# Batch one of hash attention plus SwiGLU: scaling, weight steps, hash products and one pair's loads put elsewhere in the order

## The chip, the cores and the metric

The kernel runs on one core of one Trainium2 chip. The metric is the device time of one execution in microseconds (us); the median of three executions of the kernel before is 1002.02 us.

## What is computed

The reference is two blocks in a row. The first is attention in which a query sees only the keys of its own hash bucket (4 batches, 8 heads, 768 positions, head dimension 64):

```python
q_bits = (np.einsum('bhsd,dk->bhsk', q, proj) > 0)      # 6 sign bits, k likewise
mask = q_bucket[:, :, :, None] == k_bucket[:, :, None, :]
scores = np.where(mask, scale * q @ k.T, -1e9)
attn = softmax(scores) @ v
```

The second is a SwiGLU block on x, the attention output as 3072 tokens by 512: `silu(x @ w_gate) * (x @ w_val) @ w_out`, with a hidden width of 1536. The three weight arrays come as 64-bit floats.

## The kernel before, in words

**Rows.** Heads are taken in pairs, so there are 16 pairs, n = 0 to 15, four to a batch. A *row* is half of a pair's 768 queries: row 2n is `half == 0`, row 2n + 1 is `half == 1`. The main loop (L760 to L829) goes through rows. A row has six *score units*, one for each 128 keys: `score` issues the fp32 products of q and k and the bf16 products of the sign bits into two PSUM banks (L485), and ScalarE writes their exponentials (L488). VectorE adds the exponentials up (`add`, five instructions of 128x768 per row, L514 and L518). After the units, `attend` multiplies the exponentials with v (L500) into the one-buffer PSUM tile `av`, and ScalarE copies it to xT (L507).

**Batch one** is rows 0 to 7. They hold attention only. In an even row, `total(n - 1)` comes after the second unit: TensorE sums the accumulators of the pair before into `sum` (L531; in batch one this is the same one-buffer tile as `av`), VectorE takes the reciprocal (L539), and SyncE spreads it over partitions in eight transfers (L544). `norm` then scales xT on VectorE (L551); it waits in the list `waiting`, and `finish(waiting)` issues it after the row's last unit. The next pair is prepared meanwhile by `front(n + 1)`: transposes of k and q (L387, copied by ScalarE, L390), then the *hash products* (`hash_early`, L403), whose signs ScalarE writes (L408: two for q, then four for k, which are kept in `rest` until the row's last unit). The q signs are copied to other partitions by SyncE (`spread_q`, L420: the *signs' transfer*). The hash products are issued in odd rows, after the unit c = NCH - 3 = 3.

**Weights.** The 64-bit weights are turned into fp32 on the chip while attention runs. There are 36 *pieces*: 24 of w_gate and w_val (six blocks of four), then 12 of w_out. A piece is loaded by GpSimd's queue (`load_words`, L273), scaled by ScalarE in two activations (`scale_to`, L288 and L289), and put together by VectorE in three *steps* (L302, L304, L307). After each block come four steps more (`form`, L336), which build Strassen sums; before and after them the block's matrices go to DRAM (L328, L330, L339). Twelve steps at the end build sums of w_out (L359). `prepare_on(count)` takes that many steps of this one sequence. `load_words` keeps at most a few pieces ahead of the last finished one, in buffers that are also used for other things; `scale_ahead` scales at most four pieces ahead.

**Rows 8 and later** (`gating`, from `LATE`) add the SwiGLU block of the batch before, as *atoms*: in rows 8 to 13 each holds 14 atoms, called p0 to p13 here, of two matrix products of about 1.3 us in all (`up`, L575, six PSUM banks). ScalarE takes tanh (`th`, L561), VectorE the gating (L562, L566, L579). `bring` (L318, GpSimd's queue) fetches a block from DRAM at p6, p7, p12 and p13 of each row, once TensorE has left the buffer. Rows 14 and later hold `po` atoms (w_out) as well. Between the atoms of p0 to p8 in general, `prepare_on` takes one step for each.

**Order.** Nothing is scheduled by a planner: each engine runs what is issued to it in the order of this code, and waits on semaphores. The score tiles, the transposes, the hash products and the SwiGLU products share seven PSUM banks in a ring, so that a bank is free again when its reader, seven allocations ago, is done.

Of the kernel before, what the change touches and what calls it, by code (L numbers as in the profile page):

```python
# [18 lines left out]
def kernel(  # L19
# [16 lines left out]
    NCH = S // P  # L36
# [3 lines left out]
    NP = H // 2  # L40
# [36 lines left out]
    def fetch(n, name, queue, half=None):  # L77
        b, pr = pairs[n]
        if name == "v":
            t = raws["v", n] = raw.tile([P, 2, NCH, D], FP32, tag="vraw", name="vraw")  # L80
            queue.dma_start(
                t.rearrange("p h c d -> p h (c d)"),
                v[b, 2 * pr : 2 * pr + 2].rearrange("h (p c) d -> p h (c d)", c=NCH),
            )
            return
        src = q if name == "q" else k
        if not half:
            raws[name, n] = raw.tile([P, NCH, 2, D], FP32, tag=name + "raw", name=name + "raw",
                                     bufs=1)
        t = raws[name, n]  # L90
        if n <= NP:
            cs = slice(None) if half is None else slice(half * CH, (half + 1) * CH)
            for h in range(2):
                queue.dma_start(t[:, cs, h, :],
                                src[b, 2 * pr + h].rearrange("(p c) d -> p c d", c=NCH)[:, cs, :])
            return


        blocks = t.rearrange("p c a b -> p (c a b)").rearrange(
            "p (c a d) -> p c a d", a=P // BLOCK, d=BLOCK)  # L100
        for h in range(2):
            for x in range(D // BLOCK):
                at = h * D + x * BLOCK
                queue.dma_start(  # L104
                    blocks[at : at + BLOCK],
                    src[b, 2 * pr + h][:, x * BLOCK : (x + 1) * BLOCK].rearrange(
                        "(a p c) d -> p c a d", c=NCH, p=BLOCK))

    def load(n, names):
        if n < len(pairs):  # L110
            for name in names:
                fetch(n, name, nc.sync)
# [179 lines left out]
    def scale_ahead():  # L292
        scale_to(min(progress["piece"] + 4, progress["scaled"] + 1))
# [70 lines left out]
    def prepare_on(n):  # L364
        for _ in range(n):
            next(preparing, None)
# [102 lines left out]
    LATE = NP * 2 * NCH  # L469
# [5 lines left out]
    def score(u):  # L475
        n, half, c = units[u]
        qs = slice(half * HQ, (half + 1) * HQ)
        ks = slice(c * P, (c + 1) * P)
        sc = [bank("sc")[:, 0:HQ] for _ in range(2)]
        for x, start in ((T, True), (bits, False)):  # L480
            if u < 2 and not start:
                prepare_pair(1)
            for h in range(2):
                rows = slice(h * D, (h + 1) * D)
                nc.tensor.matmul(sc[h], x["k", n][rows, ks], x["q", n][rows, qs],  # L485
                                 start=start, stop=not start)
        for h in range(2):
            nc.scalar.activation(weights(u)[:, h, 0:HQ], sc[h], AF.Exp,  # L488
                                 scale=SCALE * (OFF / 2 if n <= NP else 1.0))
# [19 lines left out]
    def add(u):  # L509
        n, half, c = units[u]  # L510
        a = weights(u)
        if c == 1:
            acc[n, half] = att.tile([P, 2, HQ], FP32, tag="acc", name="acc")
            nc.vector.scalar_tensor_tensor(out=acc[n, half], in0=weights(u - 1)[:, :, 0:HQ],  # L514
                                           scalar=S * EPS / P, in1=a[:, :, 0:HQ],
                                           op0=ALU.add, op1=ALU.add)
        elif c > 1:
            nc.vector.tensor_tensor(acc[n, half], acc[n, half], a[:, :, 0:HQ], op=ALU.add)  # L518

    def total(n):  # L520

        b, pr = pairs[n]

        ps = av_ps.tile([P, 512], FP32, tag="av", name="sum") if b == 0 else bank("sum")
        t = [acc.pop((n, half)) for half in range(2)]
        for h in range(2):
            for half in range(2):
                g = (2 * h + half) * BLOCK  # L530
                nc.tensor.matmul(ps[g : g + BLOCK, 0:HQ], ones, t[half][:, h, :],  # L531
                                 start=True, stop=True)
        if b == 0:
            space = wo.rearrange("p f m -> p (f m)")
            space = space[:, n % 2 * 3 * HQ : (n % 2 + 1) * 3 * HQ].rearrange("p (x q) -> p x q", q=HQ)
            r, t = space[:, 2, :], space[:, 0:2, :]
        else:
            r, t = t[1][:, 0, :], t[0]
        nc.vector.reciprocal(r, ps[:, 0:HQ])  # L539
        for half in range(2):  # L540
            for h in range(2):
                g = (2 * h + half) * BLOCK
                for at in (h * D, h * D + BLOCK):
                    nc.sync.dma_start(t[at : at + BLOCK, half, :], r[g : g + BLOCK, :])  # L544
        waiting.append(lambda: norm(n, t))
        if pr == NP - 1:
            push_ffn(b)
# [198 lines left out]
    rest = []  # L746

    def prepare_pair(count):
        for _ in range(count):
            rest.extend(f for f in steps.pop(0)() or [] if f)  # L750

    def finish(todo):
        while todo:
            todo.pop(0)()
# [5 lines left out]
    for u in range(0, N, NCH):  # L760
        n, half, _ = units[u]
        gating = u >= LATE
        if u == MOVE:
            progress["late"] = True
            for t in late_ring:
                nc.gpsimd.memset(t[:, :, HQ:AW], 1.0)
        for c in range(NCH):
            score(u + c)
            if u + c == 2 or not gating and half == 1 and c == NCH - 3:
                prepare_pair(1)  # L770
            if c == 1 and half == 0 and 0 < n <= NP:
                total(n - 1)
            if c:
                add(u + c)
        if n <= NP:
            finish(waiting)
            finish(rest)
        if not gating and half == 0:
            steps = front(n + 1)
        if not gating and half == 0 and u > 0:  # L780
            prepare_pair(2)
        for _ in range(1 if u else 2):
            scale_ahead()
        for c in range(NCH):
            attend(u + c)
        if not gating:
            scale_ahead()
        if half == 1:
            load(n + 2, "qkv" if gating else "v")
        elif not gating:  # L790
            prepare_pair(2 if u > 0 else 4)
            load(n + 2, "qk")
        finish(first)
        prepare_on(0 if u == LATE else 4)
        chores = []
        if half == 1 and n >= NP:
            total(n)
            if n + 1 < len(pairs):
                chores = [None] + steps.pop(0)()
        prepare_on(0 if LATE - NCH <= u <= LATE else 3)  # L800
        if not gating:
            continue
        if n + 1 < len(pairs) and half == 0:
            steps = front(n + 1)
            chores = [None, steps.pop(0), None, steps.pop(0)]

        credit += 14 if n < 2 * NP else 15.75
        end = True
        part = 0
        while atoms and (credit > 0 or not end):  # L810
            size, atom, end = atoms.pop(0)
            credit -= size
            atom()
            part += size
            if part >= 11 or u + NCH == N and part >= 6:
                finish(waiting)
                if u + NCH == N:
                    finish([first.pop(0) for _ in range(min(2, len(first)))])
            if 5 < part < 14 if u == LATE else part < 9:
                prepare_on(size)  # L820
            if 6 < part < 11 or u == LATE and part > 10:
                scale_ahead()
            for _ in range(size):
                if chores:
                    step = chores.pop(0)
                    chores.extend(step and step() or [])
        while chores:
            step = chores.pop(0)
            chores.extend(step and step() or [])  # L829
# [34 lines left out]
```

## Time and profile before

| what | us |
|---|---|
| median of 3 executions (1001.76 to 1002.82) | 1002.02 |
| the profiled execution | 1002.31 |
| its span from first to last instruction | 1000.3 |
| TensorE busy | 990.2 (99%) |
| VectorE busy | 570.7 (57%) |
| ScalarE busy | 398.4 (40%) |
| GpSimd busy | 101.5 (10%) |

The granted TensorE clock is full throughout. Shares of the whole span are averages over stages: attention alone lasts until about 114 us, weights are prepared until about 288 us, and after that VectorE is around half busy. The end of a matrix product is modelled in the profile, and a product that is held up is often shown as a longer one; lengths of whole stages tell more than the idle time.

### The profile page before, as it was taken

To read this page: it belongs to the slowest core of one execution; us is meant where nothing else is said; L and a number is where in the kernel's file an instruction comes from. 1 tells how busy PE (TensorE), PEld (TensorE's weight loads), DVE (VectorE), ACT (ScalarE), POOL (GpSimd) and SP (SyncE) were. 2 spreads that over 40 slices of the span, in tenths; PEclk is the share of its full clock that TensorE was granted. 3 is DMA by queue.
4 is the path that set the end of the run, shared out by engine and by line. 5 is a ranking of instruction groups with operands and counts; after the bars stand their busy time and mean duration, and the time that the engine had idled before them with its cause. 6 is when DMAs were issued, how large, how long until landed. Compare 5 with 4: busy or idle time off the path is not lost.

```text
span 1000.3 us, 12465 instructions
## 1 busy us (share of the span) xinstructions
PE 990.2 (99%) x4597; PEld 599.8 (60%) x4597; DVE 570.7 (57%) x892; ACT 398.4 (40%) x885; POOL 101.5 (10%) x200
## 2 busy tenths in 40 slices
PE   9999999999999999999999999999999999999998
PEld 4444455555576765555557775555556786555687
DVE  5888998887873624556564443554556442435431
ACT  6988555465323214444342223334343211222200
POOL 3222022221000000000000000000000000111000
PEclk9999999999999999999999999999999999999999
DMA  7777595885213032333331204333122012323001
GB/s 230 214 252 244 146 259 161 216 291 148 76 43 76 22 96 84 87 100 95 97 103 34 69 17 116 92 90 100 44 84 77 22 38 64 105 82 111 29 27 37
DMA packets 120749, 106.95 MB, mean 107 GB/s; under 512 B 89264, under 2 KB 104080, under 8 KB 120688
## 3 DMA queue, kind: packets, MB, share of 16 engines
q0 software_dynamic: 19104, 73.28, 22.9%
q1 hardware_dynamic: 100784, 32.67, 14.3%
q8 instruction: 36, 0.59, 0.3%
q10 hardware_dynamic: 800, 0.20, 0.1%
q14 instruction: 25, 0.20, 0.1%
HBM read 81.79 MB, written 17.30 MB: 99 GB/s over the span
## 4 chain that ended last, share of the span: by engine, by line
PE 87%; DMA 2%; DVE 1%; SPq 1%; ACT 1%; issue 1%; POOL 0%; DVEq 0%; POOLq 0%
PE up L575 43%; PE po L575 22%; PE sc L485 12%; PE av L500 9%; PE sum L531 1%; DMA words<-in_moe_w_out_dram 1%; PE hps L403 1%; SPq L104 1%; DMA wo<-wo 1%; DMA qb<-qb 0%; DMA room<-ram 0%; DVE room L359 0%; ACT A L488 0%; DVE wo L539 0%; DVE acc L518 0%
## 5 line engine op out<-in xcount | busy, mean ns | idle before, releaser
L575 PE MATMUL up<-xT,room 128*128 128x384 f32 x768 | 260.9, 488 | 0.0
L575 PEld LDWEIGHTS up<-xT,room 128*128 128x128 f32 x768 | 144.6, 190 | 106.7 <-issue 9.8
L575 PE MATMUL up<-xc,room 128*128 128x384 f32 x576 | 197.4, 486 | 0.0
L485 PE MATMUL sc<-qT,kT 64*128 64x384 f32 x768 | 161.5, 494 | 0.2 <-DVE c L562 0.2
L575 PEld LDWEIGHTS up<-xc,room 128*128 128x128 f32 x576 | 109.5, 190 | 76.3
L579 DVE TENSOR_TENSOR c<-c,up 128x384 f32<-128x384 f32 x72 | 39.8, 553 | 180.1 <-PE up L575 179.7
L518 DVE TENSOR_TENSOR acc<-acc,A 128x768 f32<-128x768 f32 x128 | 122.7, 958 | 14.4 <-ACT A L488 1.0
L318 POOL DMA_DIRECT2D room<-ram x96 | 52.4, 546 | 714.3 <-PE up L575 707.2
L488 ACT ACTIVATE A<-sc 128x384 f32<-128x384 f32 x256 | 105.6, 499 | 3.5 <-PE sc L485 3.4
L485 PEld LDWEIGHTS sc<-qT,kT 64*128 64x128 f32 x768 | 67.8, 186 | 55.5 <-issue 45.7
L710 ACT COPY o<-po 128x256 f32<-128x256 f32 x48 | 17.9, 372 | 200.5 <-PE po L575 200.5
L561 ACT ACTIVATE th<-c 128x384 f32<-128x384 f32 x72 | 37.6, 522 | 128.7 <-DVE c L562 89.2
L500 PE MATMUL av<-A,vraw 128*64 128x384 f32 (+1 forms) x512 | 88.2, 486 | 0.0
L579 DVE TENSOR_TENSOR o<-o,po 128x256 f32<-128x256 f32 x36 | 15.2, 421 | 111.6 <-PE po L575 82.5
L485 PE MATMUL sc<-qb,kb 64*128 64x384 bf16 x384 | 65.4, 323 | 1.7 <-DMA qb<-qb 1.2
L488 ACT ACTIVATE room<-sc 128x384 f32<-128x384 f32 x128 | 54.0, 495 | 32.6 <-PE sc L485 32.6
L575 PE MATMUL po<-wo,hid 128*128 128x256 f32 x288 | 66.9, 382 | 0.0
L575 PE MATMUL po<-wo,room 128*128 128x256 f32 x288 | 66.3, 379 | 0.1
L575 PE MATMUL po<-room,hid 128*128 128x256 f32 x288 | 66.1, 379 | 0.0
L500 PEld LDWEIGHTS av<-A,vraw 128*64 128x64 f32 x512 | 36.7, 137 | 46.0 <-issue 44.1
L638 ACT COPY c<-up 128x384 f32<-128x384 f32 x72 | 34.4, 478 | 69.1 <-PE up L575 69.1
L575 PEld LDWEIGHTS po<-wo,hid 128*128 128x128 f32 x288 | 54.1, 190 | 12.1 <-issue 4.9
(110 smaller groups left out, 969.4 us busy)
## 6 DMA issues: line engine op xcount, KB each, us to landing
room<-ram POOLq DMA_DIRECT2D x48, 512.0 KB, 4.8
room<-ram POOLq DMA_DIRECT2D x48, 384.0 KB, 3.9
vraw<-in_v_dram SPq DMA_DIRECT2D x16, 384.0 KB, 3.3
ram<-room POOLq DMA_DIRECT2D x12, 512.0 KB, 4.8
out_dram<-o SPq DMA_DIRECT2D x48, 128.0 KB, 1.7
room<-in_moe_w_out_dram POOLq DMA_DIRECT2D x10, 512.0 KB, 6.3
qraw<-in_q_dram SPq DMA_DIRECT2D x48, 96.0 KB, 3.2
hid<-in_moe_w_gate_dram POOLq DMA_DIRECT2D x9, 512.0 KB, 6.9
```

Of the source, the lines that this page charges most:

```text
L104: queue.dma_start(blocks[at : at + BLOCK], src[b, 2 * pr + h][:, x * BLOCK : (x + 1) * BLOCK].rearrange("(a p c) d -> p c a d", c=NCH, p=B ...
L318: nc.gpsimd.dma_start(places[k % 2][:, PARTS[go], :], ram[k % NG][:, PARTS[go], :])
L403: nc.tensor.matmul(tile_[i * BLOCK : (i + 1) * BLOCK, 0:HQ], hash_w, T[name, n][:, half * HQ : (half + 1) * HQ], start=True, stop=True)
L485: nc.tensor.matmul(sc[h], x["k", n][rows, ks], x["q", n][rows, qs], start=start, stop=not start)
L488: nc.scalar.activation(weights(u)[:, h, 0:HQ], sc[h], AF.Exp, scale=SCALE * (OFF / 2 if n <= NP else 1.0))
L500: nc.tensor.matmul(ps[h * D : (h + 1) * D, 0:width], raws["v", n][:, h, c, :], a[:, h, 0:width], start=c == 0, stop=c == NCH - 1)
L518: nc.vector.tensor_tensor(acc[n, half], acc[n, half], a[:, :, 0:HQ], op=ALU.add)
L561: nc.scalar.activation(th, g, AF.Tanh, scale=0.5)
L575: nc.tensor.matmul(ps, a, x, start=start and i == 0, stop=i == len(pairs_) - 1, skip_group_check=True)
L579: nc.vector.tensor_tensor(o, a, b, op=op)
L638: nc.scalar.copy(tile_of(g, spot), c)
L710: nc.scalar.copy(o, c)
```

## The change

Four things move, three of them in batch one.

1. `norm` (L551) of pairs 0, 1 and 2 is issued after the last unit of the odd row that follows its reciprocal, and no longer after that of the same even row. Pair 3's stays in row 8.
2. The second `prepare_on` of rows 1, 3 and 5 takes one step and no longer three: six steps fewer before row 8. In row 11 and later rows of the weights' preparation, steps are taken between the atoms p0 to p9 and no longer p0 to p7. Every step of the sequence, with its loads and scalings, comes later by six in rows 6 to 10; the six are made up two each in rows 11, 12 and 13.
3. The hash products and the q signs of rows 1, 3, 5 and 7 are issued after the third unit and no longer after the fourth.
4. The q and k loads of the sixth pair (n = 5; four transfers each) are issued in row 7, after the signs' transfer of pair 4 and just ahead of that pair's v load, and no longer in row 6.

```diff
         for c in range(NCH):
             score(u + c)
-            if u + c == 2 or not gating and half == 1 and c == NCH - 3:
+            if u + c == 2 or not gating and half == 1 and c == 2:
                 prepare_pair(1)
...
-        if n <= NP:
+        if half == 1 and n < NP or u == LATE:
             finish(waiting)
-            finish(rest)
+        finish(rest)
...
         if half == 1:
-            load(n + 2, "qkv" if gating else "v")
+            load(n + 2, "qkv" if n + 2 > NP else "v")
         elif not gating:
             prepare_pair(2 if u > 0 else 4)
-            load(n + 2, "qk")
+            if n + 2 <= NP:
+                load(n + 2, "qk")
...
-        prepare_on(0 if LATE - NCH <= u <= LATE else 3)
+        prepare_on(0 if LATE - NCH <= u <= LATE else 3 if gating or not half else 1)
...
-            if 5 < part < 14 if u == LATE else part < 9:
+            if 5 < part < 14 if u == LATE else part < (9 if u < LATE + 3 * NCH else 11):
                 prepare_on(size)
```

## The prediction

> **What bounds the kernel now.** I read the page first, then TensorE's timeline up to 320 us by rows, then what VectorE, ScalarE and the queues did where a row was longer than its like. TensorE is busy for 99% of the span, so only its stalls can be won. Its rows have fixed lengths when nothing holds them: a score stage of 36 records takes 5.05 us in the chain, an `av` stage 4.03, `sum` 0.78, an `up` stage 18.26. In batch one an odd row takes 10.85 us each time. An even row should take 10.75 (1.72 for two units, 0.78, 3.43 for four, 0.80, 4.03). The timeline (start, length, what; idle before it in brackets) gives three places:
>
> ```profile
> 62.79 1.52 PE L500 MATMUL av<-room,vraw 128*64 128x386 f32 x8 [1.67 <-DVE wo L539]
> ...
> 87.27 1.52 PE L500 MATMUL av<-room,vraw 128*64 128x386 f32 x8 [1.38 <-DVE wo L539]
> ...
> 104.41 0.32 PE L485 MATMUL sc<-qb,kb 64*128 64x384 bf16 x1 [1.17 <-DMA qb<-qb]
> ```
>
> Row 2 (31.50 to 42.60) is 0.36 over, row 4 (53.45 to 66.83) 2.63, row 6 (77.68 to 91.31) 2.88; row 8 has 1.6 too much before its `av` (109.68). In all **7.5 us**. Rows 4 and 6 are long since `sum` waits for the last addition of the row before, and `av` for the reciprocal that frees its bank. Busy times in the windows row 2+3, 4+5, 6+7 (PE, PEld, DVE, ACT, POOL):
>
> ```profile
> 31.50:53.45 21.95, 21.80 (x150) 10.12 (x148) 17.75 (x23) 20.18 (x46) 6.95 (x12) 1.00 0.69 211
> 53.45:77.68 24.23, 22.51 (x150) 10.25 (x148) 20.74 (x27) 20.17 (x46) 5.38 (x9) 1.00 0.79 265
> 77.68:102.17 24.49, 22.70 (x151) 10.26 (x149) 21.93 (x27) 20.26 (x46) 8.32 (x14) 1.00 0.85 256
> ```
>
> TensorE could do a pair in 21.6. VectorE's 20.7 to 21.9 plus its waits don't fit. Its timeline has hardly a gap from 28 to 114 us, but for `norm`, issued before its transfers land:
>
> ```profile
> 59.57 0.69 DVE L307 CUSTOM_DVE_ANT_0 room<-hid,room 128x1024 uint16<-128x1024 uint16 x1
> 60.18 2.55 DVE L539 RECIPROCAL wo<-sum 128x384 f32<-128x384 f32 x1
> ...
> 70.04 1.02 DVE L551 SCALAR_TENSOR_TENSOR xT<-xT,e,wo 128x768 f32<-128x768 f32 x1 [2.25 <-DMA wo<-wo]
> ```
>
> Later, two more stalls: row 12 begins its `av` 1.06 us late, row 13 0.9. ScalarE stood before a w_out piece, and the tanh behind it held VectorE's last bank release:
>
> ```profile
> 216.18 0.67 ACT L288 ACTIVATE wo<-words 128x512 f32<-128x512 f32 x1 [1.77 <-DMA words<-in_moe_w_out_dram]
> ...
> 244.45 0.67 ACT L288 ACTIVATE wo<-room 128x512 f32<-128x512 f32 x1 [2.79 <-DMA room<-in_moe_w_out_dram]
> 245.57 0.51 ACT L561 ACTIVATE th<-c 128x384 f32<-128x384 f32 x1
> ```
>
> **What the skill says.** The Trainium skill's Perfetto Trace Analysis, "Tensor Engine Instruction", says that ScalarE, VectorE and GpSimd work strictly first in, first out; the trace agrees: the tanh above starts right after the scaling it has nothing to do with. Its "Identifying the Most-Contended Engine" warns that matmul busy time misleads; here the stall of 7.5 us in batch one shows as under 5 us of idle time. DMA: Bandwidth & Descriptors, "Issuing engines are not separate DMA queues", says that transfers of all queues share 16 engines; in the trace a 512 KB w_out load takes 5.5 to 7.5 us by what else runs.
>
> **Batch one, step by step.** Slot lengths from VectorE's timeline (start to start): a piece's three steps 1.79, a form step 0.70, the additions of a row 5.1, reciprocal 2.47, `norm` 0.93.
>
> *Steps and `norm`.* Row 1 now ends VectorE's work at 34.34 without two form steps, so the reciprocal of row 2 follows `sum` at 34.4 and not at 35.67. Additions end at 41.9, four form steps and a piece at 46.5, row 3's additions (bound by the exponentials) at 52.1, `norm` without a wait (transfers landed near 44) at 53.0, five steps at 56.0. Before, row 3's additions ended at 55.9 and seven steps stood between them and the reciprocal at 60.18. Now row 4's `sum` waits only for ScalarE's xT copy (55.3), and the reciprocal runs from 56.2 to 58.7, ahead of `av` at 60.4. Row 4's stall falls from 2.63 to 0.2: **2.4**. The same walk through rows 5 and 6: row 6 starts at 75.3, additions of row 5 end at 73.4, `sum` at 77.0, reciprocal to 80.5 against an `av` at 82: **2.9** gone. `norm` is a move within VectorE: 0.93 less in the even row, 0.93 more in the odd one, and the waits of 2.37, 2.25 and 1.46 go. Its reader is the SwiGLU in row 8; nothing waits in between. Six steps less are 6 x 0.6 = 3.6 us of VectorE.
>
> *Hash products.* Two signs (1.15 us of ScalarE) and four products change places with one unit; no work is added. ScalarE has the q sides copied by then (in row 3: 45.0 against products at 45.95). The bank ring lets the products take the bank of a finished transpose; the next row's first unit gets their bank, and needs the k signs anyway. The cost is nothing, as ScalarE's exponentials run behind TensorE by less than the ring allows (0.4 us to spare at the tightest); without that, up to 0.6 in each odd row, the products' time.
>
> *Loads.* In row 6 the eight loads held SyncE's queue from 92.46 to 99.08, and the signs' transfer came at 99.59, landing 4.77 later. Now SyncE is free after the eight `wo` transfers, the signs come 0.8 earlier, and row 8 finds them. The eight issues go behind, some 6.6 us, with v behind them: from 91.7 to 98.7 on the new clock, landed by 102. Pair 5 is transposed near 113 there, its v is used in row 10, and the next `wo` transfers are due at 102.6. Row 8's 1.6 is gone: **1.6**. Sum of batch one **6.9, taken as 6.8** (bounds 4 and 7.5).
>
> **The price later.** Rows 8 to 10 take as many steps as before, only others, and their ends had slack: the last gating ends before TensorE asks for its bank (row 10's tanh starts 15.5 us after `up` began, and 17.6 is where a stall begins, by rows 12 and 13). Each w_out piece now stands where the piece two places earlier stood.
>
> *Row 10* scales piece 24 last. Its load waits for the block's DRAM copies and should be issued at 178.5, landing 6.3 to 7.5 later; tanh at 186.8 against a limit of 187.5. Cost 0 (0 to 1.0).
>
> *Row 11* scales piece 28 last. Its load stands behind `bring` on GpSimd's queue, as piece 30's did, and also behind the last block's copies, which start 6 us later than before. I get an issue at 208.9 against 208.68. Cost 0.2 (-0.3 to 1.5).
>
> *Row 12* ends with piece 34; before with 35. The lines of GpSimd's queue:
>
> ```profile
> 236.58 0.53 POOL L318 DMA_DIRECT2D room<-ram  x1 [6.86 <-PE up L575]
> 237.11 0.53 POOL L273 DMA_DIRECT2D room<-in_moe_w_out_dram  x1
> 237.87 0.76 POOL L318 DMA_DIRECT2D room<-ram  x1 [0.23 <-PE up L575]
> ```
>
> The load between the two `bring`s landed at 244.45. In the new order piece 34 stands behind the second, so it is issued near 238.4: 1.3 later, less if the shared engines finish all three together. Cost 1.2 (0.3 to 1.8). Piece 35 moves to row 13, where ScalarE has gaps of 1.5 to 3 us.
>
> *Rows 11 to 13* get two steps more at p8 and p9. In rows 11 and 12 VectorE waited 1.8 and 2.3 us for the late tanh: hidden. In row 13 it did not: from 266.06 to 277.6 it has gaps of 0.15 in all, and the last release (277.07) is exactly in time. Two steps of 0.62 less 0.15: cost 1.1 (0 to 1.4).
>
> *GpSimd's queue* carries the blocks' copies later too: block 2's now stand ahead of row 8's `bring` (2.5 us later, needed 10 us after), block 5's ahead of row 11's. Cover: a fetched block is used a row later.
>
> Sum: -6.8 + 0 + 0.2 + 1.2 + 1.1 = **-4.3**. The profiled run would come to 998.0; it lies 0.3 above the median, so the median to **997.8**.
>
> **Rivals.** *(A) ScalarE becomes the bound in batch one.* For it: 20.2 of 21.95 us busy in rows 2 and 3. Against it: it idles 1.6 to 3.9 us before each `av` copy. If a pair came to rest half-way, at 23.0 rather than 21.6 to 21.8, the two pairs win 1.2 and 1.5, row 8 wins 1.6, and less the price of 2.5 the gain is 1.8: 1000.2. *(B) Slower: w_out loads late in every row.* With two pieces less lead, the scalings of pieces 24, 28 and 34 each stand before a transfer; each microsecond after 16.4 us of `up` is a stall. It decides if the three rows lose more than 5.7 together beside row 13's 1.1; at 3 us each, 9.0 + 1.1 - 6.8 gives 1005.3. Against it: queue places differ by one `bring` at most. *(C) The price is absent*, because transfers finish together and VectorE's lateness is absorbed: 1002.0 - 6.8 = 995.2.
>
> **How the numbers follow.** Main case 0.62, A 0.14, B 0.10, C 0.14. A measurement of this kernel can tell about 0.2%, 2.0 us, from no change. The main case with its bounds runs from 995.8 to 1000.6, mostly under 1000.0 (0.56 of 0.62); C is faster, A on the border, with half of it above. Faster 0.74, same 0.16, slower 0.10. The range for 8 in 10 is 995.2 to 1000.8.
>
> **What would show it.** In the new profile: the reciprocals of rows 4 and 6 end before `av` is due, `av` shows no wait on L539, no wait on qb at row 8, `up` begins at 106.9 rather than 113.7; VectorE never waits before `norm` in rows 3, 5, 7. Row 12 to 14's stalls read about 1.3, 2.1 and 1.1. The forecast is wrong if even rows keep over 1 us of stall, or if ScalarE's wait before pieces 24 or 28 exceeds 3 us.

## The result, and the profile after

The changed kernel takes 998.07 us (median of 4 executions, 997.57 to 998.97) against 1001.89 for the kernel before beside it (1001.71 to 1002.82): a ratio of 0.9961, 95% interval 0.9944 to 0.9978. It is faster, by 3.8 us on the medians. The profiled executions took 997.57 and 1002.31, with spans of 995.6 and 1000.3. The forecast was 997.8.

TensorE's timeline of the changed kernel (start, length, what; idle before it would follow in brackets), at the places that answer to those shown of before:

```profile
60.17 1.52 PE L500 MATMUL av<-room,vraw 128*64 128x386 f32 x8
...
81.90 1.52 PE L500 MATMUL av<-room,vraw 128*64 128x386 f32 x8
...
97.55 0.33 PE L485 MATMUL sc<-qb,kb 64*128 64x384 bf16 x2
```

None of the three has a wait left: not on the reciprocal in rows 4 and 6, not on qb in row 8. The same pairs of rows by windows (length, then busy time and count of PE and PEld, which are TensorE's products and weight loads, DVE, which is VectorE, ACT, which is ScalarE, and POOL, which is GpSimd; then granted clock, DMA share, GB/s):

```profile
31.20:53.17 21.97, 21.80 (x150) 10.12 (x148) 19.63 (x24) 20.15 (x46) 8.72 (x15) 1.00 0.77 232
53.17:75.07 21.90, 21.81 (x151) 10.13 (x149) 20.20 (x25) 19.66 (x45) 3.31 (x5) 1.00 0.75 249
75.07:96.80 21.73, 21.73 (x151) 10.12 (x149) 19.63 (x25) 19.36 (x44) 4.30 (x8) 1.00 0.78 241
```

The pairs now all last 21.7 to 22.0 us; before, the second and third took 24.23 and 24.49. That is 2.33 and 2.76 won. The stretch from row 8's first unit to its `up` goes from 11.55 (102.17 to 113.72) to 10.07 (96.80 to 106.87): 1.48 won. In all 6.6; a further 0.3 by which the profile after is ahead arose before the first score product (it starts at 7.76 us and no longer at 8.04), which the change does not touch.

VectorE's timeline shows why:

```profile
52.06 1.01 DVE L551 SCALAR_TENSOR_TENSOR xT<-xT,e,wo 128x768 f32<-128x768 f32 x1
56.07 2.56 DVE L539 RECIPROCAL wo<-sum 128x384 f32<-128x384 f32 x1
73.65 1.01 DVE L551 SCALAR_TENSOR_TENSOR xT<-xT,e,wo 128x768 f32<-128x768 f32 x1
77.80 2.56 DVE L539 RECIPROCAL wo<-sum 128x384 f32<-128x384 f32 x1 [0.41 <-PE sum L531]
```

`norm` no longer waits, and the reciprocals end at 58.6 and 80.4, ahead of the `av` at 60.17 and 81.90. VectorE now even waits for `sum`.

SyncE's queue in row 7 and 8 has the new order: the signs' transfer, then pair 5's loads, then the `wo` transfers of row 8.

```profile
91.47 0.51 SPq L420 DMA_DIRECT2D qb<-qb  x1
92.08 3.69 SPq L104 DMA_DIRECT2D qraw<-in_q_dram  x4
95.81 3.11 SPq L104 DMA_DIRECT2D kraw<-in_k_dram  x4
...
102.12 4.99 SPq L544 DMA_DIRECT2D wo<-wo  x8
```

The price shows on ScalarE, and behind it on GpSimd's queue:

```profile
209.69 0.66 ACT L288 ACTIVATE wo<-room 128x512 f32<-128x512 f32 x1 [3.04 <-DMA room<-in_moe_w_out_dram]
...
239.03 0.68 ACT L288 ACTIVATE wo<-room 128x512 f32<-128x512 f32 x1 [3.88 <-DMA room<-in_moe_w_out_dram]
240.16 0.51 ACT L561 ACTIVATE th<-c 128x384 f32<-128x384 f32 x1
```

```profile
230.09 0.53 POOL L318 DMA_DIRECT2D room<-ram  x1 [8.19 <-PE up L575]
231.38 0.53 POOL L318 DMA_DIRECT2D room<-ram  x1 [0.76 <-DVE wo L304]
231.92 0.53 POOL L273 DMA_DIRECT2D room<-in_moe_w_out_dram  x1
```

As forecast, piece 34's load stands behind the second `bring` and lands 7.1 us after its issue, at 239.03; the tanh follows. Taken from one `av` start to the next (their free length, which is that without a wait, is 28.75, 27.35 and 28.78), the stalls at rows 12, 13 and 14 are 1.44, 1.98 and 0.58; before they were 1.07, 0.92 and 0. The `po` stage of row 14 loses 0.15 more than before. So 6.56 won, less 0.37, 1.06, 0.58 and 0.15, leaves 4.4, and with the 0.3 of the start the 4.7 between the spans.

### The profile page after: what moved, and what is told of

Same layout as the page of the kernel before. It is cut to its first block, busy times and chain, and to the rows that moved or that the text cites. A ratio compares the mean times of both kernels' runs of the same rounds, so it can differ in the third digit from the quotient of the medians.

```text
span 995.6 us, 12473 instructions
## 1 busy us (share of the span) xinstructions
PE 988.0 (99%) x4597; PEld 599.8 (60%) x4597; DVE 570.0 (57%) x892; ACT 398.5 (40%) x885; POOL 101.3 (10%) x200
## 4 chain that ended last, share of the span: by engine, by line
PE 91%; issue 3%; ACT 2%; DMA 2%; DVE 1%; POOL 0%; POOLq 0%; ACTq 0%; DVEq 0%
PE up L575 41%; PE po L575 22%; PE sc L485 14%; PE av L500 11%; DMA room<-in_moe_w_out_dram 1%; PE sum L531 1%; PE hps L403 1%; ACT A L488 1%; PE tps L387 1%; ACT kb L408 1%; DVE room L359 0%; DMA proj<-in_proj_dram 0%; DVE acc L518 0%; ACT room L488 0%; DVE c L562 0%
```

## The experiments

Stalls are read from the trace, since the longest ones also change the granted clock for a while: executions of one kernel with the mean clock at 1.000 and at 0.998 differ by some 2 us or more. "Row 8's `up`" is the start of that stage (before 113.72, changed 106.87; starts of the traces differ by up to 0.5 us). Row lengths go from one `av` start to the next. The kernels were timed in three groups on three chips, each beside the kernel before: 1002.74 us for norm, steps, loads and norm_steps; 1001.94 for no_steps, scale, early and best, and also for held on a fourth chip; 1001.76 for no_hash, own and three.

| kernel | parts | ratio to before, interval | row 8's `up` | stalls of rows 12, 13, 14 |
|---|---|---|---|---|
| norm | 1 | 1.0005, 0.9996 to 1.0015 | 114.78 | 1.03, 0.33, 0 |
| steps | 2 | 1.0054, 1.0038 to 1.0070 | 116.88 | 0.44, 2.17, 0.58 |
| loads | 3, 4 | 1.0017, 1.0008 to 1.0027 | 113.44 | 1.11, 0.50, 0 |
| norm_steps | 1, 2 | 1.0041, 1.0028 to 1.0054 | 115.22 | 1.46, 1.84, 0.58 |
| no_hash | 1, 2, 4 | 0.9960, 0.9948 to 0.9973 | 107.10 | 1.14, 2.10, 0.58 |
| no_steps | 1, 3, 4 | 0.9952, 0.9935 to 0.9969 | 107.26 | 1.39, 0.54, 0 |
| scale | 1 to 4 + scaling | 0.9915, 0.9894 to 0.9935 | 107.36 | 0, 0, 0.58 |
| early | 1 to 4, made up early | 0.9984, 0.9974 to 0.9995 | 107.39 | 2.58, 0.56, 0 |
| best | 1, 3, 4 + scaling | 0.9939, 0.9917 to 0.9960 | 107.77 | 0, 0, 0 |
| own | best, other queue | 0.9938, 0.9925 to 0.9952 | 107.55 | 0, 0, 0 |
| three | scale, three steps | 0.9918, 0.9905 to 0.9932 | 106.89 | 0.15, 0, 0 |
| held | best, copies later | 0.9977, 0.9970 to 0.9984 | 107.60 | 0, 0, 0 |

### Each part by itself: norm, steps, loads, norm_steps

The edits are the change's own hunks. norm has this one alone:

```diff
-        if n <= NP:
+        if half == 1 and n < NP or u == LATE:
             finish(waiting)
-            finish(rest)
+        finish(rest)
```

steps has these two:

```diff
-        prepare_on(0 if LATE - NCH <= u <= LATE else 3)
+        prepare_on(0 if LATE - NCH <= u <= LATE else 3 if gating or not half else 1)
...
-            if 5 < part < 14 if u == LATE else part < 9:
+            if 5 < part < 14 if u == LATE else part < (9 if u < LATE + 3 * NCH else 11):
```

loads has parts 3 and 4, and norm_steps the edits of norm and steps together:

```diff
-            if u + c == 2 or not gating and half == 1 and c == NCH - 3:
+            if u + c == 2 or not gating and half == 1 and c == 2:
...
-            load(n + 2, "qkv" if gating else "v")
+            load(n + 2, "qkv" if n + 2 > NP else "v")
...
-            load(n + 2, "qk")
+            if n + 2 <= NP:
+                load(n + 2, "qk")
```

> The kernel before with part 1 alone (norm one row later), nothing else moved. Theory T (VectorE's order sets the even rows: its waits before norm and its place ahead of the next reciprocal): row 4 keeps 0.2 us of stall, row 6 0.5, row 8 about 1.0 (SyncE's queue still has the eight loads ahead of the signs' transfer); rows 12 and 13 keep 1.06 and 0.9 and row 14 has none, since no step is moved: gain 5.3, about 996.6 us, more than the whole change. Rival S (VectorE has too much work, so that only the six steps less can help, and an idle wait taken away is refilled by the next one): rows 4 and 6 keep over 1.5 us each, 1000 us or more.

> The kernel before with part 2 alone (six steps fewer before row 8, made up in rows 11 to 13). T: VectorE still waits about 2 us before each norm; row 4 keeps 0.2, row 6 1.3, row 8 1.9; rows 12, 13, 14 cost as in the changed kernel (1.4, 2.0, 0.7, which is 2.2 more than before): net gain 1.6, about 1000.4 us. Rival S: rows 4, 6 and 8 are all but free of stalls and the time is that of the whole change, 998.

> The kernel before with parts 3 and 4 alone (hash products behind the third unit, the sixth pair's q and k loads behind the signs' transfer). T: the wait for qb at row 8 (1.17 us idle) goes, but the last addition of row 7 is ready only at 104.2 us and the reciprocal at 109.1, so that sum and av of row 8 wait in its place: gain 0.8, between 0 and 1.6, about 1001.1 us; rows 4 and 6 unchanged at 2.6 and 2.9. Rival L (the prediction's own term: the loads are worth 1.6 by themselves): 1000.3.

> The changed kernel without parts 3 and 4 (norm later and six steps fewer; hash products and loads as before). T with the queue's times: the reciprocal of row 6 ends at 80.3 and not at 87.2, so SyncE is through with its eight transfers and the eight loads near 92.3, about when the q signs are written; row 8 stalls by 0 to 0.5: 998.1 to 998.5 us. Rival L (the loads' place is what removed row 8's stall): row 8 keeps 1.2 to 1.6, 999.3 to 999.7 us.

None of the four is faster than before, where gains of 5.3, 1.6, 0.8 and some 3.5 to 4 us had been expected. norm does for rows 4 and 6 all that was expected of it: `av` begins at 60.18 and 82.13 without a wait. Row 8 then loses it again, by TensorE's timeline of norm:

```profile
103.58 0.47 PE L485 MATMUL sc<-qb,kb 64*128 64x384 bf16 x1 [5.48 <-DMA qb<-qb]
```

and SyncE's queue says why:

```profile
87.20 2.75 SPq L104 DMA_DIRECT2D qraw<-in_q_dram  x4
89.99 5.40 SPq L104 DMA_DIRECT2D kraw<-in_k_dram  x4
95.92 1.54 SPq L420 DMA_DIRECT2D qb<-qb  x1
```

Pair 5's loads start as soon as the `wo` transfers are through, the four for k take 5.40 us to issue (3.83 before), the signs' transfer gets its turn at 95.92, and it lands only near 103.5, some 7.5 us later (4.77 before). Row 8 asks for qb 5 us earlier than it used to. From row 7's `av` to row 8's it takes 17.7 us (93.01 to 110.74), 10.05 in the changed kernel. norm_steps shows a wait of 4.99 by the same queue: there the eight loads take 11.5 us to issue, the signs' transfer gets its turn at 99.13 only, and lands 3.9 later. So the loads in front of the signs' transfer, a wait of 1.17 in the kernel before, would have cost more than rows 4 and 6 brought. The theory, in which the loads hold the queue as long as before and the transfer lands as long after its issue as before, was wrong; its rival, that the qb wait takes over, was right and still too mild.

steps shows that VectorE's lower load alone does not help. Rows 4 and 6 are still 1.33 and 2.36 longer than in the changed kernel (12.35 and 13.21 from `av` to `av`, against 11.02 and 10.85), since `sum` is late for the last addition: by 1.0 in row 4, and in row 6 TensorE is shown idle for 1.34. Row 8 waits 3.00 for qb and 1.26 for additions. And then comes the whole price in rows 12 to 14.

loads takes the qb wait away and leaves rows 4 and 6 as they were. But now the reciprocal of row 8 is late, the loads (11.4 us for eight) stand in front of the `wo` transfers, and `norm` in front of `up`:

```profile
119.88 7.82 PE L575 MATMUL up<-xT,room 128*128 128x384 f32 x14 [2.95 <-DVE xT L551]
```

The parts are no sum. Each alone costs or gives nothing. Parts 1 and 4 together with either of the other two give what the change gives: that is no_hash and no_steps. (Parts 1 and 4 with neither were not run.)

### Without part 3: no_hash

The edit is the changed kernel with the hash products at `c == NCH - 3` again.

> Parts 1, 2 and 4 without part 3: the hash products stay behind the fourth score unit. Together with norm_steps (parts 1 and 2) it tells what the loads' place is worth alone, and together with the changed kernel what the products' place is worth. Theory (row 8's wait for qb is made by the loads ahead of the signs' transfer on SyncE's queue): the signs are one unit, about 0.9 us, later than in the changed kernel, the transfer starts at 92.4 instead of 91.5 and has landed when row 8 asks for qb near 98.1; no wait, up of row 8 begins at 106.9 to 107.4, the rest as in the changed kernel: within 0.5 us of it, 4.2 to 4.7 faster than before. Rival (the products' place carries the gain): row 8 keeps a wait on qb of 1 us or more.

The ratio is that of the changed kernel, 0.9960. The signs' transfer starts at 92.52, 1.05 later than with part 3 (0.23 of it is the trace's start), and has landed in time; rows 4, 6 and 8 are free of waits. The difference between no_hash and norm_steps is part 4 alone: it takes away row 8's 4.99 us. The place of the hash products gives and costs nothing that shows here.

### Without part 2: no_steps, and what part 2 is good for: best, own, held

no_steps is the changed kernel with both edits of steps undone.

> Parts 1, 3 and 4 without part 2 (every row prepares as many steps as before). The walk: rows 4, 6 and 8 need the reciprocal early, and norm a row later does that alone; VectorE has 3.6 us more to do before row 8, of which at most 0.5 us should show, at row 6. The rows 12, 13 and 14 keep the stalls of the kernel before (1.06, 0.9, none) since no piece comes later. Theory of complements (part 1 frees the even rows, part 4 keeps the qb wait away, part 2 only costs): up of row 8 begins at 107.0 to 107.5, and the kernel is 6.4 us faster than before and 1.7 faster than the changed kernel. Rival (the six steps are needed to get VectorE through rows 5 and 6): row 6 keeps over 1 us of wait, row 8's reciprocal is late, the wo transfers behind the loads hold norm, up begins at 109 or later, and the gain is under 4.5 us.

As expected, rows 4, 6 and 8 need no fewer steps: no wait up to row 8's `av`, and the stalls of rows 12 to 14 add up to 1.93 as before (1.99), against 4.00 with part 2. But the gain is 3.7 us on the medians and not 6.4, and the end of the rival's chain came true: the reciprocal is not late and `up` begins at 107.26, but the `wo` transfers stand behind the loads, and after its first ten products `up` waits 2.06 us for `norm`. With the clock falling behind it (below), the row is 4.0 longer in this trace (27.32 from `up` to the next `av`, 23.30 in the changed kernel). best, where the clock held, shows the wait alone: 25.78, so 2.48 longer. What part 2 takes later (2.2 with `po`), it gives here; in time the two kernels cannot be told apart.

best has one more edit, scale's (below):

> Parts 1, 3 and 4, without part 2, and the last scaling of a row moved ahead of the next row's attention from row 11 on. Theory: the gain of no_steps (6.4) and, since no step is late, the stalls of rows 12 and 13 as before (1.06 and 0.9) gone as well: 8.4 us faster than the kernel before, the ratio 0.9917, some 3.7 us faster than the changed kernel. Rival (part 2 is needed in batch one, or VectorE's own work holds the later rows): under 6 us faster than before.

Its rows 12 to 14 are free, but row 8's wait puts it 2.1 behind scale in span (994.8 and 992.7), and the ratio is 0.9939 and not 0.9917. TensorE's and VectorE's timelines of best, and SyncE's queue:

```profile
113.47 4.78 PE L575 MATMUL up<-xT,room 128*128 128x384 f32 x14 [2.20 <-DVE xT L551]
```

```profile
112.40 1.02 DVE L551 SCALAR_TENSOR_TENSOR xT<-xT,e,wo 128x768 f32<-128x768 f32 x1 [4.32 <-DMA wo<-wo]
```

```profile
92.53 0.51 SPq L420 DMA_DIRECT2D qb<-qb  x1
93.14 7.15 SPq L104 DMA_DIRECT2D qraw<-in_q_dram  x4
100.33 4.43 SPq L104 DMA_DIRECT2D kraw<-in_k_dram  x4
...
105.92 5.08 SPq L544 DMA_DIRECT2D wo<-wo  x8
```

The reciprocal began at 100.47, near the changed kernel's 99.53 (0.5 of it is the trace's start), so VectorE's six steps are not what is late. The loads take 11.6 us to issue instead of 6.8. GpSimd sends block 2's copies to DRAM from 88.8 to 92.9 in no_steps (89.3 to 93.4 in best), and from 97.28 on in the changed kernel. Is it SyncE's order or the full engines? own sends pair 5's q and k loads from GpSimd's queue:

```diff
             for name in names:
-                fetch(n, name, nc.sync)
+                fetch(n, name, nc.gpsimd if n == NP + 1 and name != "v" else nc.sync)
```

> Parts 1, 3 and 4 and the last scaling of a row moved ahead of the next row's attention from row 11 on (the kernel best), with one change: the eight q and k loads of pair 5 go to GpSimd's queue instead of SyncE's. In best SyncE needed 11.6 us to issue them (93.1 to 104.8), the wo transfers of row 8 came behind them at 105.9 and norm stood 2.2 us in the way of up. Theory Q (SyncE's queue order): SyncE is free when the reciprocal starts at 100.5, the wo transfers are issued from there or from 103, norm starts 2 us earlier or more, up has no wait; 2 us faster than best, some 10 faster than before. Theory E (the 16 engines are full with the loads and block copies, whoever issues them): the wo transfers land no earlier than in best, norm keeps at least 1.5 of its 2.2 us, and nothing is gained; GpSimd's later copies could even be late.

SyncE was free, issued the `wo` transfers at 102.80 as soon as the reciprocal was done, and `norm` still waited 3.73 us for them (VectorE's timeline of own):

```profile
111.56 1.02 DVE L551 SCALAR_TENSOR_TENSOR xT<-xT,e,wo 128x768 f32<-128x768 f32 x1 [3.73 <-DMA wo<-wo]
```

`up` waits 1.59 instead of 2.20, and the row is 0.6 shorter: theory E in the main, and what the Trainium skill says in DMA: Bandwidth & Descriptors, "Issuing engines are not separate DMA queues": another issuing queue is no other set of engines. The `wo` transfers landed 4.0 to 7.4 us after their issue, in best 1.9 to 3.9. From 100 to 108 us the DMA share is 1.12 and 0.98 in two windows of 4 us. It is not quite clean, for GpSimd's two w_gate loads came at 100.4 and 100.9 in this order.

held leaves SyncE's queue as in best, and issues the block's copies in row 8:

```diff
             nc.gpsimd.dma_start(places[k % 2][:, PARTS[go], :], ram[k % NG][:, PARTS[go], :])
+        if k == 3 and go == 0:
+            while held:
+                held.pop(0)()
...
-        for pair, i in enumerate(group):
+        def copy(pair, i):
...
+        def send(f, pair, i):
+            if n == 2:
+                held.append(lambda: f(pair, i))
+            else:
+                f(pair, i)
```

> The kernel best (parts 1, 3, 4, every row with its full steps, last scaling moved from row 11 on), with one change: the six copies of form block 2 to DRAM, which GpSimd issues from 88.8 to 92.9 in best, are held back and issued in row 8 behind the second bring, near 117 (their first reader is row 9's bring, near 149). Theory D (in best it is the block's copies that meet pair 5's loads and then the wo transfers of row 8 in the 16 engines, and the six steps that the changed kernel leaves out before row 8 help only by moving the copies later): SyncE's q and k loads take about 7 us to issue as in the changed kernel instead of 11.6, the wo transfers land some 2 us earlier, norm waits about 1.4 us instead of 4.3, up of row 8 has no wait on xT, nothing is paid later; 2.2 faster than best and level with the kernel three. Rival V (the 3.6 us of VectorE's work that the six steps are, or the two w_gate loads on GpSimd): up keeps at least 1.5 of its 2.2 us, and the kernel is level with best.

It changes what is computed in one point: piece 16 is scaled into the block's buffer before the late copies read it, so block 2 is stored with that piece's values in part. No instruction is left out. In row 8 it is what theory D said; SyncE's and VectorE's timelines of held:

```profile
92.96 3.80 SPq L104 DMA_DIRECT2D qraw<-in_q_dram  x4
96.81 3.09 SPq L104 DMA_DIRECT2D kraw<-in_k_dram  x4
...
102.88 5.00 SPq L560 DMA_DIRECT2D wo<-wo  x8
```

```profile
109.29 1.02 DVE L567 SCALAR_TENSOR_TENSOR xT<-xT,e,wo 128x768 f32<-128x768 f32 x1 [1.38 <-DMA wo<-wo]
```

The loads take 6.9 us, `norm` waits 1.38, `up` does not wait, and VectorE did its six steps all the same. From 104 to 108 us the DMA share is 0.38, in best 1.16. So **part 2 helps batch one by moving the block's copies (with the w_gate load behind them, which is 4.0 us earlier in held than in best) out of the way of pair 5's loads and row 8's `wo` transfers, and not by sparing VectorE.** What the copies and what the w_gate load are worth each, held does not tell. "Nothing is paid later" was wrong: ScalarE's next scaling overwrites the buffer that the late copies read, and waits for them; the exponentials of row 9 stand behind it.

```profile
127.60 0.67 ACT L288 ACTIVATE room<-hid 128x512 f32<-128x512 f32 x1 [6.90 <-DMA ram<-room]
```

Row 9's scores wait 2.73, and the row loses 3.6 in all: more than the 2.48 won. The timed ratio is worse again than that, since most of its executions had the lower mean clock.

### Where the price comes from: scale, early, three

scale takes the last scaling of rows 11 and later out from before the third tanh; the next row's `scale_ahead` does it:

```diff
-            if 6 < part < 11 or u == LATE and part > 10:
+            if 6 < part < (11 if u < LATE + 3 * NCH else 10) or u == LATE and part > 10:
```

> The changed kernel, but from row 11 on ScalarE scales its last w_out piece not at the tenth SwiGLU atom of a row, before the third tanh, but ahead of the next row's attention. Theory (the scaling that waits for its load holds the tanh, and the tanh VectorE's last bank release): the third tanh of rows 11 and 12 starts without the 3.04 and 3.88 us waits, the stalls of 1.44 and 2.0 us at rows 12 and 13 go, row 14's 0.6 stays; 3.4 us faster than the changed kernel, 8.1 faster than before. Rival (VectorE is late by its own work): the tanh starts earlier, yet the release stays, and the stalls keep over half of their length; under 1.5 us faster than the changed kernel.

Both waits are gone and the stalls at rows 12 and 13 with them, to the hundredth: 28.75 and 27.34 from `av` to `av`. ScalarE's timeline of scale in rows 11 and 12:

```profile
208.49 0.52 ACT L561 ACTIVATE th<-c 128x384 f32<-128x384 f32 x1 [1.35 <-DVE c L562]
...
235.35 0.52 ACT L561 ACTIVATE th<-c 128x384 f32<-128x384 f32 x1 [1.14 <-DVE c L562]
```

The tanh starts when VectorE hands it its input, and piece 34 loses nothing by being scaled at 243.71. Row 14's 0.6 stays. Against the changed kernel it is 3.4 faster from row 11 on.

The traces of all the kernels give the same rule. A stall at row 12 or 13 is what the third tanh of the row before starts later than 17.67 us after that row's `up` began, within 0.02 us: 18.74 goes with 1.07 and 18.59 with 0.92 in the kernel before, 19.11 with 1.44 and 19.66 with 1.98 in the changed kernel, 18.11 with 0.44 and 19.84 with 2.17 in steps. Where the tanh starts earlier there is no stall, but for the 0.15 of three.

early makes the six steps up in earlier rows:

```diff
-            if 5 < part < 14 if u == LATE else part < (9 if u < LATE + 3 * NCH else 11):
+            if 5 < part < 14 if u == LATE else part < (9 if u >= LATE + 4 * NCH else 11):
```

> The changed kernel with the six steps made up in rows 9 to 11's place, that is two each in the first rows that have room (rows up to 11 instead of rows 11 to 13). Theory (each row's stall is set by the load of the piece that it scales last): row 13's stall falls from 2.0 back to 0.9 and row 14's 0.6 to none, while row 12's grows from 1.44 to about 2.3, since piece 30's load then stands behind the second bring on GpSimd's queue; in all 0.8 us faster than the changed kernel, 5.5 faster than before. Rival (the two steps cost VectorE's time wherever they stand): rows 9 to 11 show stalls of 0.5 to 1 each, and it is no faster than the changed kernel.

Row 14 came out as said, row 12 near it (2.58), and row 13 better (0.56). But row 11 lost 5.8 us, which was not expected: the steps of row 9 bring piece 25 into row 10's last scaling, whose load was issued at 175.17 and took 9.0 us to land.

```profile
184.17 0.66 ACT L288 ACTIVATE wo<-room 128x512 f32<-128x512 f32 x1 [5.12 <-DMA room<-in_moe_w_out_dram]
185.28 0.51 ACT L561 ACTIVATE th<-c 128x384 f32<-128x384 f32 x1
```

The tanh starts 21.79 us after `up` began, which makes a stall of 4.1; the other 1.7 are the granted clock, which stood at half from 188.0 to 191.5. The theory held, a row's stall is set by the load of the piece that it scales last, but the expectation had not applied it to row 10.

three is scale with the six steps made up three each in rows 11 and 12:

```diff
-            if 5 < part < 14 if u == LATE else part < (9 if u < LATE + 3 * NCH else 11):
+            if 5 < part < 14 if u == LATE else part < (12 if LATE + 3 * NCH <= u < LATE + 5 * NCH else 9):
```

> The kernel scale, but the six steps are made up three each in rows 11 and 12 instead of two each in rows 11, 12 and 13, so that row 13 has none. Theory (row 14's 0.6 us comes from the two steps in row 13, where VectorE has no gap): row 14 begins without a stall, rows 12 and 13 stay within 0.2 since VectorE has room there now that the tanh does not wait; 0.6 us faster than scale, 9.1 faster than before. Rival (the additions behind the last piece make row 14 late whatever is added in row 13, or rows 11 and 12 have no room for a third step): a stall of 0.5 or more remains in rows 12 to 14, and nothing is gained over scale.

Row 14's 0.58 is gone and so is the 0.14 of its `po`, row 12 has 0.15: 0.57 less in the rows. The two extra steps in row 13 were its cause. At 993.73 us against 1001.76, three is 8.0 us faster than the kernel before, and 4.3 faster than the changed kernel by the ratios (0.9918 and 0.9961); scale and three can't be told apart by their ratios, by the rows of the traces three is ahead by 0.57.

## Why the prediction was right, point by point

**Rows 4, 6 and 8** were forecast at 2.4, 2.9 and 1.6 and came to 2.33, 2.76 and 1.48. The walk along VectorE held to 0.2 us (reciprocal at 56.07 for 56.2, `norm` without a wait), and `up` began at 106.87 for 106.9.

**Which part brings it** was only half right. That `norm` frees rows 4 and 6 is shown by norm. But the prediction credited the loads' place with 1.6, what row 8 loses in the kernel before. Without it the changed kernel would lose about 8 us in row 8 (norm, norm_steps), all that rows 4 and 6 gain and more. The step that failed is the silent one, that what stands ahead of row 8 in SyncE's queue takes as long as before when everything around it comes 5 us earlier. The loads held the queue for 8.2 us in norm and 11.5 in norm_steps instead of 6.6, and the signs' transfer behind them landed 7.6 and 3.9 us after its issue instead of 4.8. The six steps were counted as "3.6 us of VectorE"; batch one does not need them (no_steps), and they help by the block's copies (held). Their queue-side effect was named only as harmless: "a fetched block is used a row later". The total came out since in the changed kernel both collisions are avoided; that part 2 would be needed for it was not foreseen, and was luck.

**Hash products** at nothing: right, and shown by no_hash.

**Row 10** at nothing: right (27.35 from `av` to `av`, its free length), with the tanh 16.74 us after `up` began. **Row 11's last piece** +0.2: measured +0.37. **Row 12's last piece** +1.2: measured +1.06, by the mechanism named, piece 34 behind the second `bring`; scale shows it as the cause. Both loads were issued where the walk had put them, within 0.2 us (201.89 and 231.92 on the new clock). The prediction had named a wait of ScalarE of over 3 us before pieces 24 or 28 as a sign of being wrong; it was 2.02 and 3.04, so the sign was just met, though the row lost little more than before: it was set too low.

How the two terms split is less sure than these figures look, for the landing of a load differs from trace to trace. In the four traces with part 2 and the scaling in its old place (changed, steps, norm_steps, no_hash) row 12's stall is 0.44 to 1.46 and row 13's 1.84 to 2.17; in the four with neither (before, norm, loads, no_steps) they are 1.03 to 1.39 and 0.33 to 0.92. By the means the first term is nothing and the second 1.45. Their sum, 1.4, is what was forecast. The 5.5 to 7.5 us that the prediction gave for a w_out load were too narrow: in the trace of before the loads issued from 170 to 240 us took 3.7 to 9.4 us to land.

**Row 13's two steps** +1.1: this term was mis-sized. The stall is 0.58, with 0.15 in `po`. VectorE's last release came 20.42 us after `up` began in the kernel before (277.07), and 21.34 after it in the changed kernel (272.58): 0.92 later rather than 1.09. And "exactly in time" was not so: by the difference of the two, some 0.34 of slack was there, which the reading of the trace had missed. (That the modelled ends of the products hid it is likely, and not shown.) three shows that the two steps are the cause.

**Sum**: -4.3 forecast, -4.4 by rows. That they are so near is in part luck: batch one came 0.2 short, and row 13's steps cost 0.4 less. Two slips are in the arithmetic: 998.0 less 0.3 is 997.7, and the chances given for a faster kernel add up to 0.77 and not 0.74. Rival A (ScalarE the bound at 23 us a pair) is out, with pairs at 21.7 to 22.0; rival B (late loads in every row) is out in the changed kernel, but early shows that it was near: one piece whose load took 9.0 us to land cost 5.8 us, 1.7 of them by the clock. Rival C (no price) is out.

## What to carry to other kernels

When a stage gets faster, its transfers are asked for earlier and meet others: work out anew where each transfer stands in its queue and what else the DMA engines carry then, and don't take the time that it holds the queue, or its landing time, from the trace of before. Put nothing that waits for a load in front of an instruction that holds a buffer of the bounding engine; moving one such scaling brought 3.4 us, where the whole change brought 4.4. Test the parts of a change in combination, since parts that each bring nothing alone may be the gain together.

## What was not expected of the hardware

TensorE's granted clock fell to half after a stall of a few microseconds, and stayed there for 3.4 us (no_steps, early) or 6.8 us (norm, norm_steps, loads). In norm, by windows of 1 us (columns as above, the granted clock is the third from the right):

```profile
100.00:101.00 1.00, 0.00 (x0) 0.00 (x0) 0.03 (x1) 0.00 (x0) 0.06 (x1) 0.91 1.05 234
101.00:102.00 1.00, 0.00 (x0) 0.00 (x0) 0.00 (x0) 0.00 (x0) 0.00 (x0) 0.50 1.09 301
...
106.00:107.00 1.00, 1.00 (x8) 0.00 (x0) 0.00 (x0) 0.52 (x2) 0.00 (x0) 0.50 0.00 0
107.00:108.00 1.00, 1.00 (x8) 0.60 (x6) 0.84 (x1) 0.00 (x0) 0.00 (x0) 0.68 0.00 0
```

TensorE had stopped near 98.1; the clock fell near 100.8, the products resumed at 103.58, and until 107.6 they ran at half speed, which costs some 2 us more. The Trainium skill's TensorE: Matmul & The Clock Gate, "What's actually happening", gives an idle window of about 3.4 us for this, one that runs freely of the kernel. The traces here agree on the half and on its coming and going between executions, and the two lengths are once and twice this window; but they show the fall after shorter stalls too: 2.06 us in no_steps (at half from 113.8 to 117.2 us), 2.95 in loads (119.2 to 126.0) and 3.21 in early, while best had 2.20, held 2.73 and steps 3.00 without it in the executions profiled. The mean clock was below full (0.998 or less) in every execution of norm and norm_steps, in 17 of 22 of early, 17 of 20 of held, 6 of 22 of loads, 5 of 6 of steps, 2 of 6 of best, 1 of 8 of no_steps and 1 of 4 of the changed kernel, and in none of scale, three, own and no_hash. Waits in the traces don't explain all of it: the kernel before, with no wait over 1.7 us in its trace, had it in 5 of 38 executions beside norm. So a wait of over 2 us in this kernel can cost 1.5 to 3.3 us beyond itself, and not in every execution.

The eight q and k loads took 6.6 to 6.9 us of SyncE's queue in the kernel before, the changed kernel and held, and 11.6 in best, where the block's copies ran beside them: from 92 to 100 us the DMA share is 0.94 and 1.04 in best, and 0.35 and 0.80 in held (windows of 4 us). The signs' transfer took 4.8 us to land in the kernel before, 7.6 in norm and 3.9 in norm_steps.
